# Tying the second layer's weight decoding to places in the product stream, and a reordered, two-queue ending, in a scan plus two-layer MLP kernel

## Chip, cores and metric

One core of one Trainium2 chip runs the whole program in one launch. The metric is the device time of one execution in microseconds (us); for the kernel before it is 641.49 us, the median of 3 runs (641.38 to 641.57).

## The reference

A decayed linear-attention scan over 4 sequences of 768 steps (8 heads of 32) gives 3072 tokens of 256 numbers. Two MLP layers follow:

```python
x = attn_out.transpose(0, 2, 1, 3).reshape(3072, 256)
xn = x / sqrt(mean(x * x, -1) + 1e-6) * rms_g          # layer 1, d_ff 1536
x = (silu(xn @ w_gate) * (xn @ w_val)) @ w_out
r = maximum(x @ w_in, 0.0)                              # layer 2, d_ff 2048
out = (s * (r * r) + b) @ w_out2
```

The weights arrive as 64-bit floats and are turned into fp32 on the chip ("decoding"). To keep fp32 accuracy on fast passes, both factors of a product are split into a high and a low part (`hi`, `lo`), and three products are summed.

## The kernel before, in words

The program is not issued as it is written. A recording class, `Plan`, collects every engine call with its predecessors; `issue` (L322) then sorts them by list scheduling with the planner's own prices and hands each engine its instructions in that order. So all work shows as line L356 in the profile, the warm-up products of TensorE as L352, and groups are told apart by tile names. Each engine then runs its list strictly in that order and waits by semaphores.

The stages: the scan runs in pairs of chunks (tiles `ab`, `a_sb`, `m`, `y`, `xn`, `ss`, `rs`, `xth`, `xtl`). Layer 1 works on 7 blocks of tokens (4, 4, 4, 5, 5, 5, 5 chunks of 96); for each block, 12 tiles `m` of the hidden width are made by `hidden1` (tiles `h`, `s`, `hi`, `lo`) and multiplied into the accumulators `o`. Block 0 uses plain fp32 products (`hidden1_plain`, weights `w1f`) while the weights of layer 1 are decoded by `decode1`. The 16 tiles of layer 2's weights are decoded by `decode2` (L715), called once for every third `m` of blocks 2 to 5 (L1039). One decoding of a layer-2 tile is five VectorE operations of 512 columns (`e<-raw`, `raw<-raw`, `w2f<-raw`, `e<-e,sg`, `w2f<-w2f,e`), two ScalarE operations (`e`, `sg`) and one GpSimd sum (`w_sum`). Nothing but data and buffers says when they run; the planner may put them before the place in the program text where they are called.

Layer 2 works on 6 groups of 512 tokens with seven products in place of eight (`seven`, `seven_out`, L923), which collect in seven accumulators of 256 columns in four PSUM banks (`soon`, `late`; tiles `acc` and `o`). At a group's end `seven_out` puts the seven together on VectorE into `res`, and `store` (L822) applies `s * ... + bias` to 512 columns on ScalarE into `ob` and sends the pieces to `out_t`, all on SyncE's queue (SP). The last group has six such stores.

TensorE's idle stretches at the start are filled by `issue` with products of constants (L352), so many as the planner's clock finds room for.

Of the kernel before, what the change touches and what calls it, by code (L numbers as in the profile page):

```python
# [8 lines left out]
F32 = mybir.dt.float32  # L9
# [7 lines left out]
AF = mybir.ActivationFunctionType  # L17
ALU = mybir.AluOpType

P = 128  # L20
# [5 lines left out]
SEQ = 768  # L26
CPB = SEQ // CH
UT = 2 * CH
NPAIR = 2
# [13 lines left out]
N2 = 512  # L43
# [14 lines left out]
class Plan:  # L58
# [23 lines left out]
    def __init__(self, nc):  # L82
        self.nc, self.ops, self.clock, self.pace = nc, [], 0.0, False
        self.seen, self.rings, self.masks, self.before, self.heads = {}, {}, {}, {}, {}
        self.closed, self.sent, self.turns, self.bundle = set(), None, False, None
        self.now_free = True
        self.fresh, self.after, self.held, self.squares = False, None, None, None
        for e in ("tensor", "vector", "scalar", "gpsimd", "sync"):
            setattr(self, e, Engine(self, e))

    def add(self, eng, fn, args, kw):
        op = dict(eng=eng, fn=fn, args=args, kw=kw, preds={}, paced=self.pace, i=len(self.ops))
        op["dur"] = self.price(eng, fn, args, kw)
        if fn == "dma_start":
            op["eng"] = self.DMA[eng]
        reads = [a for k, a in kw.items() if k not in self.WRITES] + list(args)
        writes = [a for k, a in kw.items() if k in self.WRITES]
        if args and fn in self.FIRST_OUT:
            writes.append(reads.pop(len(kw) - len(writes)))
        for a in reads:  # L100
            self.touch(op, a, False)
        for a in writes:
            self.touch(op, a, True)
        if self.turns:

            if self.sent is not None:
                op["preds"].setdefault(self.sent["i"], -self.DMA_LEAD - self.sent["dur"])
            self.sent = op
        if self.after is not None:
            op["preds"].setdefault(self.after, 0.0)  # L110
        op["clock"] = self.clock
        op["group"] = kw["out"].name if fn == "matmul" and not self.pace else None
        if self.fresh and op["eng"] == "tensor":
            op["dur"] += self.SWITCH[fn]
            self.fresh = False
        if self.bundle is not None and op["eng"] == "tensor":
            op["group"] = self.bundle
            self.join(op)
        if self.pace:
            self.clock += op["dur"]  # L120
        self.ops.append(op)


# [247 lines left out]
def scan_glu_relu2(ctx: ExitStack, tc: tile.TileContext, bc, xr, aa, cst, w1, w2, gn, sv, bv, out):  # L371
    nc = Plan(tc.nc)
    PS = bass.MemoryType.PSUM

    const = ctx.enter_context(tc.tile_pool(name="const", bufs=1))
# [9 lines left out]
    xt_p = ctx.enter_context(tc.tile_pool(name="xt", bufs=2))  # L385
    x1_p = ctx.enter_context(tc.tile_pool(name="x1", bufs=3))
    s_p = ctx.enter_context(tc.tile_pool(name="s", bufs=3))
    hl_p = ctx.enter_context(tc.tile_pool(name="hl", bufs=LAG + 1))
    ps_h = ctx.enter_context(tc.tile_pool(name="ps_h", bufs=2, space=PS))
    ps_o = ctx.enter_context(tc.tile_pool(name="ps_o", bufs=1, space=PS))  # L390
    ps_y = ctx.enter_context(tc.tile_pool(name="ps_y", bufs=2, space=PS))
# [1 line left out]
    cst_sb = const.tile([P, 4], F32, name="cst_sb")  # L393
    raw_bc = const.tile([P, 2, 3, 2 * R + NST], F32, name="raw_bc")
    a_sb = const.tile([P, SLOTS, NH, AW], F32, name="a_sb")
    sb = const.tile([P, 6], F32, name="sb")
    s_sb, b_sb, bias_sb, g_sb = sb[:, 0:1], sb[:, 1:2], sb[:, 2:4], sb[:, 4:6]
    delta = const.tile([P, NH, AW], F32, name="delta")
    ident = const.tile([P, P], F32, name="ident")
# [289 lines left out]
    def flat(t):  # L689
        return t.rearrange("p a b -> p (a b)")  # L690
# [24 lines left out]
    def decode2(m):  # L715
        raw = w2_p.tile([P, 4 * P], I64, tag="w2", name="raw2")
        words(raw, w2[m])
        w2f[m] = w2f_p.tile([P, 4, P], F32, tag="w2f", name="w2f")
        decode(raw, flat(w2f[m]), 4 * P)
        if m:  # L720
            last = w2f[0][:, 2:4] if m == 1 else w2_sum
            nc.gpsimd.tensor_tensor(out=w2_sum, in0=last, in1=w2f[m][:, 2:4], op=ALU.add)
# [96 lines left out]
                        if lo < hi:  # L819
                            yield lo - a, to + lo - at, hi - lo  # L820

    def store(g, t, o):  # L822
        res = s_p.tile([P, N2], F32, tag="s", name="ob")
        nc.scalar.activation(
            out=res, in_=o, func=AF.Identity, scale=s_sb, bias=bias_sb[:, t:t + 1]
        )
        todo = sorted(runs(g * N2, (g + 1) * N2))
        while todo:
            at, to, n = todo.pop(0)
            same = [r for r in todo if r[2] == n]  # L830
            more = []
            if same:
                step, jump = same[0][0] - at, same[0][1] - to
                while (at + (len(more) + 1) * step, to + (len(more) + 1) * jump, n) in todo:
                    more.append((at + (len(more) + 1) * step, to + (len(more) + 1) * jump, n))
                    todo.remove(more[-1])
            k = len(more) + 1
            src = res[:, at:at + n]
            dst = out[t * P:(t + 1) * P, to:to + n]
            if more:  # L840
                src = bass.AP(src.tensor, src.offset, [list(src.ap[0]), [step, k], [1, n]])
                dst = bass.AP(dst.tensor, dst.offset, [list(dst.ap[0]), [jump, k], [1, n]])
            nc.sync.dma_start(out=dst, in_=src)

    combined = {}

# [25 lines left out]
    def bias_products():  # L872
        ps = ps_y.tile([P, 2, 512], F32, tag="y", name="bias")
        ones = nc.nc.const_aps.tensor(1.0, (P, 2), F32)
        for t in range(2):
            nc.tensor.matmul(out=ps[:, t, 0:2], lhsT=w2_sum[:, t], rhs=ones, start=True, stop=True)
        for t in range(2):
            nc.vector.tensor_scalar_mul(bias_sb[:, t:t + 1], ps[:, t, 0:1], b_sb)

# [43 lines left out]
    def seven_out(j, q, parts):  # L923
        n = HALF
        if q == 0:
            o_t[j, 2] = new_sums(j)
        sums, soon, late = o_t[j, 2]
        last = q == F2 // 2 - 1
        for k, ((wh, wl), (hi, lo)) in enumerate(zip(combined[q], parts)):
            three(sums[k], wh, wl, hi, lo, q == 0 and k in (0, 2, 3, 5), last and k in (1, 2, 4, 6))  # L930
        if not last:
            return
        res = xt_p.tile([P, 4, n], F32, tag="xth", name="res")
        side = xt_p.tile([P, 2, n], F32, tag="xtl", name="side")
        two = slice(0, 4, 3)
        first, second, third = (
            t[:, 0:2 * n].rearrange("p (s n) -> p s n", s=2) for t in (soon[0], late[0], late[1])
        )
        one = soon[1][:, None, 0:n].to_broadcast([P, 2, n])
        nc.scalar.copy(out=side, in_=first)  # L940
        nc.vector.tensor_tensor(out=res[:, two], in0=one, in1=side, op=ALU.subtract)
        nc.vector.tensor_tensor(out=res[:, two], in0=second, in1=res[:, two], op=ALU.add)
        nc.vector.tensor_tensor(out=res[:, 0], in0=res[:, 0], in1=third[:, 0], op=ALU.subtract)
        nc.vector.tensor_tensor(out=res[:, 1], in0=third[:, 1], in1=side[:, 0], op=ALU.add)
        store(j, 0, res[:, 0:2].rearrange("p s n -> p (s n)"))
        nc.vector.tensor_tensor(out=res[:, 3], in0=third[:, 1], in1=res[:, 3], op=ALU.add)
        nc.vector.tensor_tensor(out=res[:, 2], in0=side[:, 1], in1=third[:, 0], op=ALU.subtract)
        store(j, 1, res[:, 2:4].rearrange("p s n -> p (s n)"))

    def drain(n):  # L950
        while len(pending) > n:
# [4 lines left out]
                      in_=aa.rearrange("c (u f) -> (c u) f", u=2))  # L956
# [7 lines left out]
        out=ident, in_=ident, compare_op=ALU.not_equal, fill=1.0, base=0,  # L964
# [70 lines left out]
    for i, (layer, j, m) in enumerate(plan):  # L1035
        if (layer, j) == (1, 1):
            split1(m)
        if layer == 1 and 2 <= j < NBLK - 1 and m % 3 == 0:
            decode2((j - 2) * 4 + m // 3)  # L1039
        late = m if layer == 1 and j == NBLK - 1 else F1 + m // 2 if (layer, j) == (2, 0) and m % 2 == 0 else None  # L1040
        if late == 0:
            split_rows(0)
            bias_products()
        for q in range(F2 // 2):
            if late == (max(2 * q, 1) if q < 7 else F1 + 2):
                combine(q)
        if layer == 2:
            if m == 0 and (g := j + 1) * N2 < 2 * NPAIR * SEQ:
                split_rows(g)
            if m % 2 == 0:  # L1050
                seven(j, m // 2)
                drain(LAG)
            continue
        hidden1(j, m)
        drain(LAG)
        for (i0, n0), (i1, n1) in zip(marks, marks[1:]):
            if i0 <= i < i1:
                tokens_to(n0 + -(-(n1 - n0) * (i + 1 - i0) // (i1 - i0)))
# [74 lines left out]
```

## Time and profile before

| | |
|---|---|
| median of 3 runs | 641.49 us |
| the profiled execution | 641.33 us |
| its span, first to last instruction | 639.2 us |
| TensorE matmul busy | 623.8 us (98%) |
| TensorE weight load busy | 555.5 us (87%) |
| VectorE (DVE) busy | 482.3 us (75%) |
| ScalarE (ACT) busy | 437.3 us (68%) |
| GpSimd (POOL) busy | 60.5 us (9%) |

The span is from the first to the last instruction; 2.1 us of the execution lie outside it. Matmuls are pipelined, so "busy" of TensorE (PE) counts stretches in which at least one is in flight; a lost moment shows as an idle time before a group or as a larger step from one start to the next. PEclk is the granted clock of TensorE as a share of full speed.

### The profile page before, as it was taken

The page shows a single profiled execution, that of the slowest core. Times are in us where ns is not written, and L with a number is a line of the kernel's source. Part 1 is how long each engine was busy: PE and PEld are TensorE (multiplying, and loading weights), DVE is VectorE, ACT ScalarE, POOL GpSimd, SP SyncE. Part 2 cuts the span into 40 slices and gives each one's busy share as a digit, 9 for nine tenths or more (in the row PEclk, how much of TensorE's full clock was granted, in tenths as well). Part 3 has the DMA queues.
Part 4 walks back from the last instruction along what each step waited for, and adds up shares of the span by engine and source line. Part 5 has one row for each costly group of instructions (what it writes and reads, how often), then busy time and mean ns, then how long its engine had stood idle before and what let it go on. Part 6 is the DMA issues. An engine that isn't in the chain of part 4 may idle for free.

```text
span 639.2 us, 12930 instructions
## 1 busy us (share of the span) xinstructions
PE 623.8 (98%) x4959; PEld 555.5 (87%) x4959; DVE 482.3 (75%) x979; ACT 437.3 (68%) x928; POOL 60.5 (9%) x88
## 2 busy tenths in 40 slices
PE   8899999999999999999999999999999999999995
PEld 7799999889988888888888888999999999999995
DVE  7999999999754635544554559787888888888794
ACT  4697566676644534553554569888889888888884
POOL 3000022235210000000001220000000000000000
PEclk9899999999999999999999999999999999999999
DMA  7868235553202203210100000001010010000101
GB/s 226 241 200 252 56 100 158 139 132 89 56 1 49 61 5 62 65 36 4 41 1 2 0 1 1 2 4 31 2 33 2 1 34 1 26 8 2 34 1 33
DMA packets 33694, 35.00 MB, mean 55 GB/s; under 512 B 14048, under 2 KB 30048, under 8 KB 33632
## 3 DMA queue, kind: packets, MB, share of 16 engines
q1 hardware_dynamic: 33376, 33.98, 20.2%
q8 instruction: 39, 0.64, 0.4%
q10 hardware_dynamic: 256, 0.20, 0.1%
q14 instruction: 23, 0.19, 0.1%
HBM read 30.90 MB, written 3.25 MB: 53 GB/s over the span
## 4 chain that ended last, share of the span: by engine, by line
PE 82%; DVE 11%; ACT 3%; issue 2%; DMA 0%; DVEq 0%; SPq 0%; ACTq 0%
PE h L356 46%; PE o L356 19%; PE acc L356 12%; PE y L356 4%; DVE w2f L356 2%; DVE e L356 2%; DVE s L356 1%; DVE lo L356 1%; DVE a_sb L356 1%; DVE raw L356 1%; DVE m L356 1%; DVE w1l L356 1%; PE o L352 1%; DVE xtl L356 1%; DVE w1f L356 1%
## 5 line engine op out<-in xcount | busy, mean ns | idle before, releaser
L356 ACT ACTIVATE s<-h 128x512 f32<-128x512 f32 (+2 forms) x168 | 96.2, 573 | 55.5 <-PE h L356 53.3
L356 ACT CAST hi<-s 128x256 fp32r<-128x256 f32 (+2 forms) x168 | 78.2, 473 | 69.2 <-DVE s L356 67.6
L356 PE MATMUL h<-x1h,w2h 128*128 128x512 f32 x384 | 119.5, 392 | 0.0
L356 DVE TENSOR_TENSOR lo<-s,hi 128x256 fp32r<-128x256 f32 (+2 forms) x168 | 87.9, 524 | 27.8 <-ACT hi L356 27.2
L356 PE MATMUL h<-xth,w1h 128*128 128x480 f32 (+1 forms) x288 | 107.2, 373 | 1.2 <-DVE s L356 0.8
L356 PE MATMUL h<-xtl,w1h 128*128 128x480 f32 (+1 forms) x288 | 106.6, 370 | 0.0
L356 PE MATMUL h<-xth,w1l 128*128 128x480 f32 (+1 forms) x288 | 106.4, 369 | 0.0
L356 PE MATMUL acc<-hi,w2c 128*128 128x256 f32 x448 | 82.4, 281 | 0.0
L356 DVE TENSOR_TENSOR s<-h,s 128x480 f32<-128x480 f32 (+1 forms) x72 | 44.5, 618 | 49.6 <-PE h L356 45.6
L356 PEld LDWEIGHTS h<-x1h,w2h 128*128 128x128 f32 x384 | 69.0, 188 | 11.8
L356 PE MATMUL h<-x1l,w2h 128*128 128x512 f32 x192 | 75.1, 391 | 0.0
L356 PEld LDWEIGHTS acc<-hi,w2c 128*128 128x128 f32 x448 | 71.6, 190 | 2.7
L356 DVE TENSOR_TENSOR added<-s 128x256 f32<-128x256 f32 x144 | 57.1, 421 | 10.0 <-ACT s L356 9.2
L356 PE MATMUL acc<-lo,w2c 128*128 128x256 f32 x224 | 63.2, 282 | 0.0
L356 PEld LDWEIGHTS h<-xth,w1h 128*128 128x128 f32 x288 | 54.1, 188 | 9.6 <-DVE s L356 2.6
L356 ACT ACTIVATE s<-s 128x512 f32<-128x512 f32 x96 | 59.6, 632 | 1.1
L356 PEld LDWEIGHTS h<-xtl,w1h 128*128 128x128 f32 x288 | 54.1, 188 | 6.3 <-issue 1.0
L356 PEld LDWEIGHTS h<-xth,w1l 128*128 128x128 f32 x288 | 54.1, 188 | 6.0 <-issue 0.3
L356 DVE TENSOR_TENSOR lo<-added,hi 128x768 fp32r<-128x768 f32 x48 | 46.0, 958 | 14.5 <-ACT hi L356 14.4
L356 PE MATMUL o<-hi,w1h 128*128 128x480 f32 (+1 forms) x144 | 53.2, 369 | 0.5 <-ACT hi L356 0.5
L356 PE MATMUL o<-lo,w1h 128*128 128x480 f32 (+1 forms) x144 | 52.7, 366 | 0.8 <-DVE lo L356 0.8
L356 PE MATMUL o<-hi,w1l 128*128 128x480 f32 (+1 forms) x144 | 53.2, 369 | 0.0
(98 smaller groups left out, 1099.6 us busy)
## 6 DMA issues: line engine op xcount, KB each, us to landing
raw<-in_w SPq DMA_DIRECT2D x12, 768.0 KB, 5.1
raw<-in_w SPq DMA_DIRECT2D x16, 512.0 KB, 4.3
a_sb<-a_scr SPq DMA_DIRECT2D x28, 196.0 KB, 4.2
xh<-in_xr SPq DMA_DIRECT2D x60, 48.0 KB, 1.9
raw_bc<-in_bc SPq DMA_DIRECT2D x56, 32.0 KB, 2.2
raw_bc<-in_bc SPq DMA_DIRECT2D x112, 16.0 KB, 2.6
out_t<-ob SPq DMA_DIRECT2D x14, 96.0 KB, 1.8
out_t<-ob SPq DMA_DIRECT2D x6, 144.0 KB, 1.9
```

What stands on the lines that cost most here:

```text
L352: self.nc.tensor.matmul(out=idle, lhsT=ones, rhs=ones, start=True, stop=True)
L356: getattr(engine, op["fn"])(*op["args"], **op["kw"])
```

## The change

1. A call of `decode2` sets `nc.floor` to the last product recorded before it (`nc.latest`, set only for the layers' products). While it is set, every VectorE and ScalarE operation gets that product as a predecessor, so no part of a decoding on these two engines can be planned before its place among layer 1's products. Loads and GpSimd sums are not tied.
2. At a group's end ScalarE scales first and VectorE adds last: four ScalarE operations of 256 columns write `s * part + bias` into `res`, and four `scalar_tensor_tensor` operations add `+s` or `-s` (the new column `minus_s`) times the last two accumulators. `ob` and its two ScalarE operations of 512 columns are gone; stores read `res`, which gets a pool of its own.
3. The last group's second half is stored from ScalarE's queue in place of SyncE's.

```diff
+        self.now_free, self.floor, self.latest = True, None, None
...
-        if self.after is not None:
-            op["preds"].setdefault(self.after, 0.0)
+        for i in (self.after, self.floor if eng in ("vector", "scalar") else None):
+            if i is not None:
+                op["preds"].setdefault(i, 0.0)
...
         if self.pace:
             self.clock += op["dur"]
+            self.latest = op["i"]
...
+    res_p = ctx.enter_context(tc.tile_pool(name="res", bufs=1))
...
-    sb = const.tile([P, 6], F32, name="sb")
+    sb = const.tile([P, 7], F32, name="sb")
+    minus_s = sb[:, 6:7]
...
-    def store(g, t, o):
-        res = s_p.tile([P, N2], F32, tag="s", name="ob")
-        nc.scalar.activation(
-            out=res, in_=o, func=AF.Identity, scale=s_sb, bias=bias_sb[:, t:t + 1]
-        )
+    def store(g, t, res):
+        queue = nc.scalar if t and (g + 1) * N2 == 2 * NPAIR * SEQ else nc.sync
...
-            nc.sync.dma_start(out=dst, in_=src)
+            queue.dma_start(out=dst, in_=src)
...
+        nc.vector.tensor_scalar(out=minus_s, in0=s_sb, scalar1=-1.0, scalar2=None, op0=ALU.mult)
...
-        res = xt_p.tile([P, 4, n], F32, tag="xth", name="res")
+        res = res_p.tile([P, 4, n], F32, tag="res", name="res")
...
-        nc.vector.tensor_tensor(out=res[:, 0], in0=res[:, 0], in1=third[:, 0], op=ALU.subtract)
-        nc.vector.tensor_tensor(out=res[:, 1], in0=third[:, 1], in1=side[:, 0], op=ALU.add)
-        store(j, 0, res[:, 0:2].rearrange("p s n -> p (s n)"))
-        nc.vector.tensor_tensor(out=res[:, 3], in0=third[:, 1], in1=res[:, 3], op=ALU.add)
-        nc.vector.tensor_tensor(out=res[:, 2], in0=side[:, 1], in1=third[:, 0], op=ALU.subtract)
-        store(j, 1, res[:, 2:4].rearrange("p s n -> p (s n)"))
+        parts = [(side[:, 0], 1, s_sb), (res[:, 0], 0, minus_s), (side[:, 1], 0, minus_s), (res[:, 3], 1, s_sb)]
+        for k in (2, 1, 0, 3):
+            t = 0 if k < 2 else 1
+            nc.scalar.activation(
+                out=res[:, (1, 0, 2, 3)[k]], in_=parts[k][0], func=AF.Identity, scale=s_sb, bias=bias_sb[:, t:t + 1]
+            )
+        for t in range(2):
+            for k in (2 * t, 2 * t + 1):
+                to = res[:, (1, 0, 2, 3)[k]]
+                nc.vector.scalar_tensor_tensor(
+                    out=to, in0=third[:, parts[k][1]], scalar=parts[k][2], in1=to, op0=ALU.mult, op1=ALU.add
+                )
+            store(j, t, res[:, 2 * t:2 * t + 2].rearrange("p s n -> p (s n)"))
...
         if layer == 1 and 2 <= j < NBLK - 1 and m % 3 == 0:
+            nc.floor = nc.latest
             decode2((j - 2) * 4 + m // 3)
+            nc.floor = None
```

The planner sorts everything anew with these predecessors, so the order changes in places that the diff does not touch. Three places follow.

First, VectorE at the start of the program, from the first `w1f` weights to the second (`raw_135` of before is `raw_138` of the change, the second tile; `a_sb<-ab` is the scan of a chunk, `m<-y` a scan product, `h` the hidden tile of block 0). Before:

```order
L356 TENSOR_TENSOR w1f<-w1f,e 128x768
L356 SCALAR_TENSOR_TENSOR a_sb<-ab,delta 128x392
L356 TENSOR_SCALAR raw_135<-raw_135 128x768
L356 TENSOR_SCALAR e<-raw_136 128x768
L356 TENSOR_TENSOR e<-e,sg 128x768
L356 TENSOR_TENSOR h_154<-h,h_154 128x192
L356 SCALAR_TENSOR_TENSOR w1f<-raw_135 128x768
L356 TENSOR_TENSOR m<-y,a_sb 128x8x48
L356 TENSOR_SCALAR raw_136<-raw_136 128x768
L356 TENSOR_TENSOR w1f<-w1f,e 128x768
```

And now:

```order
L358 SCALAR_TENSOR_TENSOR a_sb<-ab,delta 128x392
L358 TENSOR_TENSOR e<-e,sg 128x768
L358 COPY held<-rs 128x2
L358 SCALAR_TENSOR_TENSOR w1f<-raw_137 128x768
L358 TENSOR_SCALAR e<-raw_138 128x768
L358 TENSOR_TENSOR w1f<-w1f,e 128x768
L358 TENSOR_SCALAR raw_138<-raw_138 128x768
L358 TENSOR_SCALAR e<-raw_139 128x768
L358 TENSOR_TENSOR e<-e,sg 128x768
L358 SCALAR_TENSOR_TENSOR w1f<-raw_138 128x768
L358 TENSOR_TENSOR w1f<-w1f,e 128x768
L358 TENSOR_TENSOR h_157<-h,h_157 128x192
```

The scan now stands ahead of the first weights, and `h`, `m` and a mask of the third tile stand behind the second. On TensorE the constant products ahead of the first transposes (`y<-ident,xn`) grow from 23 to 31, and 12 new ones stand between the first tile's products and the second's; from the products `y<-xh,m` of the next pair on, TensorE's list is for a while the old one.

Second, VectorE among layer 1's products (`s`, `lo` are the pair that `hidden1` needs of it for each tile, `xtl` a scan result, `w2h` a split of a decoded tile). Before, at the last tiles of block 1:

```order
L356 TENSOR_TENSOR w2h<-w2f,w2h 128x256
L356 TENSOR_TENSOR s<-h,s 128x384
L356 TENSOR_TENSOR e<-e,sg 128x512
L356 TENSOR_SCALAR raw_585<-raw_585 128x512
L356 SCALAR_TENSOR_TENSOR xtl<-y,sb,xth 128x2x48 x2
L356 TENSOR_TENSOR w2h<-w2f,w2h 128x256
L356 TENSOR_TENSOR lo<-s,hi 128x384
L356 SCALAR_TENSOR_TENSOR xtl<-y,sb,xth 128x2x48 x2
L356 SCALAR_TENSOR_TENSOR w2f<-raw_585 128x512
L356 TENSOR_SCALAR raw_616<-raw_616 128x512
```

And now, at the end of block 2 (its last `s`, `lo` of 384 columns):

```order
L358 TENSOR_TENSOR s<-h,s 128x384
L358 TENSOR_SCALAR e<-raw_487 128x512
L358 TENSOR_TENSOR lo<-s,hi 128x384
L358 TENSOR_SCALAR raw_487<-raw_487 128x512
L358 SCALAR_TENSOR_TENSOR w2f<-raw_487 128x512
L358 TENSOR_TENSOR e<-e,sg 128x512
L358 TENSOR_TENSOR w2f<-w2f,e 128x512
L358 TENSOR_TENSOR s<-h,s 128x480
L358 TENSOR_TENSOR lo<-s,hi 128x480
L358 TENSOR_TENSOR s<-h,s 128x480
L358 TENSOR_TENSOR lo<-s,hi 128x480
L358 TENSOR_TENSOR s<-h,s 128x480
```

Of the 16 decodings none stands before block 2 now: there is one for every third `hi`/`lo` pair, from the 12th pair to the 57th, where before all 16 stood between the 2nd pair and the 21st.

Third, ScalarE's last rows, before:

```order
L356 COPY side<-acc 128x512
L356 ACTIVATE ob<-res,sb 128x512 x2
```

And now:

```order
L358 COPY side<-acc 128x512
L358 ACTIVATE res<-side,sb 128x256 x2
L358 ACTIVATE res<-res,sb 128x256 x2
L358 DMA out_t<-res 128x32
L358 DMA out_t<-res 128x2x96
L358 DMA out_t<-res 128x2x144
```

Two of the four scalings need only `side`; the other two need the sum of VectorE's second addition. ScalarE issues its three stores behind its last scaling. VectorE's last four rows, `res<-o_1467,sb,res 128x256`, work on the third, first, second and fourth quarter of `res` in this order; SyncE keeps three stores.

## Rows read from the trace of the kernel before

**Rows 1.** Busy time by stretch: us, then busy us (count) by engine, PEclk, DMA share, GB/s.

```profile
100.00:180.00 80.00, 77.43 (x758) 70.37 (x758) 74.65 (x158) 54.91 (x140) 30.68 (x28) 1.00 0.44 110
180.00:320.00 140.00, 140.00 (x1247) 117.41 (x1247) 68.86 (x137) 63.34 (x157) 5.03 (x8) 1.00 0.17 37
420.00:632.00 212.00, 212.00 (x1351) 192.52 (x1350) 177.73 (x356) 182.16 (x339) 0.00 (x0) 1.00 0.05 13
```

**Rows 2.** Waits of PE from 100 to 180 us: total, times, longest.

```profile
PE h L356 <- DVE s L356: 0.8, 2, 0.4
PE o L356 <- DVE lo L356: 0.8, 1, 0.8
PE o L356 <- ACT hi L356: 0.5, 1, 0.5
```

**Rows 3.** Timeline of PE around one such wait: start, duration, operation, idle before.

```profile
122.02 0.34 PE L356 MATMUL o<-hi,w1l 128*128 128x384 f32 x1
122.20 0.33 PE L356 MATMUL o<-lo,w1h 128*128 128x384 f32 x1
123.04 0.44 PE L356 MATMUL o<-hi,w1h 128*128 128x384 f32 x1 [0.50 <-ACT hi L356]
```

**Rows 4.** Groups of DVE from 80 to 165 us, the decodings: busy, mean ns, idle before.

```profile
L356 DVE SCALAR_TENSOR_TENSOR w2f<-raw 128x512 f32<-128x512 uint32 x16 | 11.2, 698 | 0.0
L356 DVE TENSOR_TENSOR w2f<-w2f,e 128x512 f32<-128x512 f32 x16 | 11.0, 690 | 0.0
...
L356 DVE TENSOR_SCALAR raw<-raw 128x512 int32<-128x512 int32 x15 | 7.2, 477 | 0.0
...
L356 DVE TENSOR_TENSOR e<-e,sg 128x512 bf16<-128x512 bf16 x16 | 6.6, 413 | 0.0
L356 DVE TENSOR_SCALAR e<-raw 128x512 uint16<-128x512 uint16 x15 | 6.3, 417 | 0.0
```

**Rows 5.** Timeline of DVE at the start: three operations between first and second weights.

```profile
15.46 0.97 DVE L356 TENSOR_TENSOR_SCAN a_sb<-ab,delta 128x392 f32<-128x392 f32 x1
...
17.73 0.35 DVE L356 TENSOR_TENSOR h<-h,h 128x192 f32<-128x192 f32 x1
...
18.86 0.55 DVE L356 TENSOR_TENSOR m<-y,a_sb 128x384 f32<-128x384 f32 x1
```

**Rows 6.** Timeline of PE at the start: the groups that waited.

```profile
20.89 1.54 PE L356 MATMUL h<-xth,w1f 128*128 128x192 f32 x8 [1.01 <-DVE w1f L356]
24.14 1.12 PE L356 MATMUL y<-xh,m 64*64 64x32 f32 x32 [1.71 <-DVE m L356]
...
33.20 2.87 PE L356 MATMUL h<-xth,w1f 128*128 128x192 f32 x16 [0.54 <-ACT xth L356]
```

**Rows 7.** Busy time by stretch at the start, columns as in rows 1.

```profile
12.00:16.00 4.00, 3.25 (x43) 2.76 (x41) 3.97 (x8) 3.83 (x9) 0.27 (x1) 1.00 0.83 187
20.00:24.00 4.00, 1.54 (x8) 1.27 (x8) 4.00 (x7) 2.53 (x4) 0.00 (x0) 1.00 0.74 226
26.00:30.00 4.00, 4.00 (x40) 3.94 (x37) 2.91 (x7) 2.18 (x7) 1.33 (x1) 0.57 1.01 232
```

**Rows 8.** Timeline of the end, all engines, after the last but one addition.

```profile
631.43 0.69 DVE L356 TENSOR_TENSOR res<-o,res 128x512 f32<-128x512 f32 x1
...
632.92 1.53 ACT L356 ACTIVATE ob<-res,sb 128x512 f32<-128x512 f32 x2 [2.34 <-DVE res L356]
633.13 0.41 DVE L356 TENSOR_TENSOR res<-side,o 128x256 f32<-128x256 f32 x1
633.76 3.00 SPq L356 DMA_DIRECT2D out_t<-ob  x6
```

**Rows 9.** A group of DVE with a pointer scalar, by form (mean ns after the comma).

```profile
L356 DVE SCALAR_TENSOR_TENSOR xtl<-y,sb,xth 128x96 fp32r<-128x96 f32 x56 | 14.4, 310 | 6.6 <-ACT xth L356 6.2
```

**Rows 10.** DMA issues: count, KB each, median us from issue to landing.

```profile
out_t<-ob SPq DMA_DIRECT2D x14, 96.0 KB, 1.8
...
xh<-in_xr ACTq DMA_DIRECT2D x4, 48.0 KB, 3.1
```

More of the change, by code (lines that the diff above doesn't have):

```diff
@@ L85, in __init__ @@
         self.closed, self.sent, self.turns, self.bundle = set(), None, False, None
-        self.now_free = True
+        self.now_free, self.floor, self.latest = True, None, None
         self.fresh, self.after, self.held, self.squares = False, None, None, None
```

## Prediction

> **What bounds the kernel now.** I read the page first: TensorE (PE) matmuls cover 98% of the span, so only what PE waits for, and what stands before its first and behind its last product, can move the time. Then busy time by stretch [rows 1]. From 180 to 320 us and from 420 to 632 us PE is busy all the time, with VectorE (DVE) at 49% (68.86 of 140) in the one and 84% (177.73 of 212) in the other. From 100 to 180 us it loses 2.57 us, and there DVE is full (74.65 of 80). Then PE's list of waits for that stretch [rows 2]: it waits for `s` and `lo` of DVE and `hi` of ScalarE (ACT), the three steps by which `hidden1` hands a tile on. Last the start [rows 5 to 7] and the end [rows 8].
>
> **Middle: the decodings move.** What fills DVE in that stretch is the decoding of layer 2's weights: five operations a tile, 0.698 + 0.690 + 0.477 + 0.413 + 0.417 = 2.70 us, 16 tiles, about 43 us from 80 to 165 us [rows 4]. `hidden1`'s own steps queue among them, as the order before shows. With the floor these 43 us leave the stretch up to block 2 and come back as one tile at every third `hi`/`lo` pair, up to the end of block 5.
>
> What it gives: the waits of rows 2 sum to 0.8 + 0.8 + 0.5 = 2.1 us in four waits. Idle time understates a wait, because matmuls overlap: the step from 122.20 to 123.04 is 0.84 us, while 0.50 is listed as idle and the regular step there is 0.18 (122.02 to 122.20), so 0.84 − 0.50 − 0.18 = 0.16 comes on top [rows 3]. So 2.1 + 4 × 0.16 = 2.7 us. Of the 0.47 us idle that these four do not hold (2.57 − 2.1) I count 0.4 as curable: 3.1 us at most. All of it goes if DVE is no longer full.
>
> What it costs: where the decodings go, DVE had 49%. About 12 tiles fall between 180 and 320 us: 12 × 2.70 = 32 us, which makes (68.86 + 32) / 140 = 72%. In layer 2 DVE runs at 84% and ACT at 86% and PE loses nothing [rows 1]; that is the cover. If it fails, one decoding can cost what one wait for `s` costs, 0.4 + 0.16 = 0.56 us [rows 2, 3]. I put two such brushes in, 0.3 us after what slack hides. Middle: **−2.8 us**, between −3.1 and −1.0.
>
> GpSimd's sums (`w_sum`) move with the decodings; it has 31 us of work in 80 [rows 1], and the chain that ends in it is wanted only when layer 2 starts. The 16 loads of raw tiles on SyncE's queue (SP) move too, behind the same buffers; SP waits there, and nothing but loads stands behind them. `minus_s` is one column. All three at nothing.
>
> **Start: a by-product.** The planner's new order puts the scan of 0.97 us ahead of the first weights [rows 5], so the first products come up to 0.97 us later; constant products fill the gap. Between the first and the second weights the scan, `h` (0.35) and `m` (0.55) are gone [rows 5]: 1.87 us less, so the second weights come at least 1.87 − 0.97 = 0.9 us sooner, and the wait of 1.01 us for them at 20.89 us [rows 6] nearly closes. But PE's next group, at 24.14 us, waits 1.71 us for `m` of DVE [rows 6], and up to there DVE has the same work in both orders and no idle time (4.00 of 4 busy from 20 to 24) [rows 7]. So PE is no earlier there: 0, with +0.7 and −0.2 as bounds.
>
> What can change is the clock. From 26 to 30 us it stands at a mean of 0.57 of full, after PE had been busy for 1.54 us of the 4 from 20 to 24 [rows 7]; that is (1 − 0.57) / 0.5 × 4 = 3.4 us at half speed, 1.2 GHz in place of 2.4. It costs at most 1.7 us of products. After 3.25 of 4 (81%, constant products included, 12 to 16 us) it had stayed up [rows 7]. In the new order PE's second group comes some 1.3 us sooner, 12 constant products run before it, and the spread `ab` and the first `o` products follow it: I count some 2.8 us busy of the 4 from 20 to 24, 70%, nearer to the 81% than to the 39%. I take it that the clock stays up. The half-speed products lie on the chain to the wait at 33.20 us (`h`, the ACT steps behind it, the transposes, `xth`) [rows 6]; from there DVE is nearly full again and gives part back. Of 0 to −1.7 I take the middle: **−0.8 us**.
>
> **End.** Before [rows 8]: the second addition ends at 631.43 + 0.69 = 632.12 us; four additions follow on DVE, up to 633.13 + 0.41 = 633.54; two scalings of 512 columns on ACT, 1.53 us from 632.92 on; then six stores on SP from 633.76 to 636.76, 0.50 each, and 2.47 us later the span ends. Now:
>
> - ACT scales the first two quarters while DVE adds; these are hidden. The scaling of `res` (first and fourth quarter) starts at 632.12. A scaling of 256 columns was not seen; it lies between 0.38 (half of 1.53 / 2) and 0.77 us. It has half the columns but the same start-up; I take 0.55. They end at 632.7 and 633.2.
> - DVE's four `scalar_tensor_tensor` of 256 columns: like the addition, 0.41 [rows 8], plus something for the pointer. The nearest row with one takes 0.310 us for 96 columns [rows 9], so 160 columns more, at 0.41 / 256 us each at most, give 0.57 as the upper end. I take 0.45, 0.40 from start to start. The first quarter waits for ACT (632.7), so the four end at 632.6, 633.15, 633.55 and 633.95.
> - SP stores from 633.2: third issue at 634.2, done 634.7. ACT's queue starts behind its last scaling, 633.25; its third store waits for 633.95 and is done at 634.75. Both are done some 2.0 us before 636.76.
>
> If a store on ACT's queue lands as on SP's (1.8 us [rows 10]), the span ends 2.0 us sooner. The only row for ACT's queue has 3.1 us [rows 10], at the start, with the DMA engines busy; that would take 1.3 back. I take the row for the same stores, and 0.1 for issuing from two engines: **−1.9 us**, between −0.6 and −2.2.
> The Trainium skill (DMA: Bandwidth & Descriptors, "Issuing engines are not separate DMA queues") says that DMAs from all engines run on the same 16 DMA engines, and that several issuing engines only save the time of issuing, "usually small relative to the DMA itself". By its first half ACT's stores land like SP's, and the sum keeps −1.9; by ACT's own row it would be −0.6. Its second half does not fit here: six issues in a row took 3.00 us, against 1.8 for a landing [rows 8, 10].
>
> At the other five group ends the same operations run beside PE, which loses nothing there; ACT has some 4 × 0.55 in place of 1.53 us each time, 0.7 us more a group: nothing. Cover: the 14% that ACT is idle; without it, 5 × 0.7 = 3.5 us.
>
> **Sum** on the profiled execution (641.33 us, span 639.2): −2.8 − 0.8 − 1.9 = −5.5, so 635.8 us. The median of the runs is 0.16 us above that execution; I leave it out.
>
> **Rivals.**
>
> 1. *The clock falls as before.* For it: PE still waits for `m` shortly before 24.14 us. Then the start gives 0: 636.6 us.
> The Trainium skill (TensorE: Matmul & The Clock Gate, Part 1) has the throttled state as the default, which activity lifts, and says that the moment of change varies from run to run. By that rule the fall may stay in some runs and not in others; the granted clock here shows one fall after a thin stretch.
> 2. *The middle was not the decodings'.* `s`, `hi` and `lo` also queue behind scans, `xtl` and splits, which stay. If two thirds of the waits remain, the middle gives 1.0: 637.6 us.
> 3. *A new wait at every decoding (slower).* The five operations now stand beside blocks 2 to 5 at 16 fixed places, ahead of `s` or `lo` in DVE's list; the order shows one `e<-raw` between `s` and `lo`. If each place costs PE one wait of 0.56 us, that is 9.0 us against 3.1 + 0.8 + 1.9 = 5.8 of gains: 644.5 us. It decides from 5.8 / 16 = 0.36 us a place on. Against it: 84% of DVE without a wait in layer 2.
> 4. *The end does less than it says.* ACT's queue is slow to land, or the last scaling holds ACT's stores back: −0.6 there, 637.1 us.
>
> **How the numbers follow.** Forecast 0.45; rival 1 0.25; rival 2 0.12; rival 4 0.11; rival 3 0.07. The range: below, the forecast with every term near its good end (3.1 + 1.7 + 2.2 = 7.0, so 634.3); above, rivals 1 and 2 together, 638.4. That leaves out rival 3 and the worst sums. A measurement of this kernel can tell about 0.2% (1.3 us) from no change. All cases but rival 3 are faster by more; of rival 3's 0.07 some 0.02 end within the 1.3 us, and sums of two rivals add 0.03 there: faster 0.90, same 0.05, slower 0.05.
>
> **What would show it.** Middle: PE busy all of 100 to 180 us, no wait for `s`, `hi`, `lo`, DVE under 85% there and above 65% from 180 to 320; rival 3 shows as waits for `s` or `lo` beside `w2f` rows from 160 to 310. Start: granted clock 1.00 from 26 to 30; the group that waited at 33.20 some 0.8 us sooner. End: from the second addition's end to the span's end 5.2 us in place of 7.1, with stores on two queues. I would be wrong if PE's waits in the middle stay with DVE no longer full, or if the second addition is no longer what the end hangs on.

## The result, and the profile after

The changed kernel takes 633.81 us (median of 4 runs, 633.74 to 633.88) against 641.47 us (641.38 to 641.57): ratio 0.9883, 95% interval 0.9867 to 0.9898. The forecast was 635.8 us, with 634.3 as the lower end. So it was right that it is faster, but the gain is 7.7 us in place of 5.7, half a microsecond below the range.

I cut both traces at three products of TensorE (PE): the first with `w1h` (layer 1's high part), the first with `w2h` (layer 2) and the last one. Timeline of PE, before:

```profile
77.77 0.47 PE L356 MATMUL h<-xth,w1h 128*128 128x384 f32 x1
...
377.30 0.40 PE L356 MATMUL h<-x1h,w2h 128*128 128x512 f32 x1
```

and after:

```profile
78.04 0.47 PE L358 MATMUL h<-xth,w1h 128*128 128x384 f32 x1
...
371.64 0.40 PE L358 MATMUL h<-x1h,w2h 128*128 128x512 f32 x1
```

| stretch (us) | before | after | difference | forecast |
|---|---|---|---|---|
| start, to the first `w1h` product | 77.77 | 78.04 | +0.27 | −0.8 |
| middle, `w1h` to `w2h` | 299.53 | 293.60 | −5.93 | −2.8 |
| layer 2, to the last product | 254.51 | 254.32 | −0.19 | 0 |
| end, from the last product on | 7.42 | 5.86 | −1.56 | −1.9 |
| span | 639.23 | 631.82 | −7.41 | −5.5 |

The middle gained twice what was forecast; the start gained nothing. Before, four products of block 0 (`o<-h,w1f`) come behind the first cut that now come ahead of it; cut at block 0's last product, with the same work on both sides, the two differences are +0.19 and −5.85. The middle in busy time by stretch, columns as in [rows 1]:

```profile
100.00:180.00 80.00, 80.00 (x785) 75.18 (x784) 56.96 (x124) 49.51 (x128) 6.27 (x9) 1.00 0.35 83
180.00:320.00 140.00, 140.00 (x1262) 117.42 (x1261) 95.42 (x194) 78.71 (x190) 19.34 (x23) 1.00 0.26 63
```

PE has no idle time left from 100 to 180 us (2.57 before), and the list of PE's waits for that stretch, [rows 2] before, is empty. VectorE (DVE) falls from 74.65 to 56.96 of 80 us and rises from 68.86 to 95.42 of 140 (68%; 72% was forecast). GpSimd (POOL) falls with it, from 30.68 to 6.27 us. Groups of DVE and POOL by form, 80 to 165 us; first before:

```profile
L356 DVE TENSOR_TENSOR lo<-s,hi 128x384 fp32r<-128x384 f32 x22 | 15.1, 685 | 0.0
...
L356 POOL TENSOR_TENSOR w_sum<-w_sum,w2f 128x256 f32<-128x256 f32 x13 | 17.8, 1372 | 38.9 <-DVE w2f L356 38.8
```

then after (`w_sum` there from 80 to 330 us):

```profile
L358 DVE TENSOR_TENSOR lo<-s,hi 128x384 fp32r<-128x384 f32 x23 | 12.7, 552 | 6.3 <-ACT hi L358 6.3
...
L358 POOL TENSOR_TENSOR w_sum<-w_sum,w2f 128x256 f32<-128x256 f32 x14 | 12.9, 924 | 118.6 <-DVE w2f L358 118.6
```

The same `lo` took 685 ns on the mean before and 552 after. I had not looked at this before the result. In the trace of before, 16 of the 22 took 541 to 556 ns and six took 996 to 1092. In each of those six a `w_sum` of GpSimd was already under way when `lo` began; `lo` ended some 0.42 us after that sum. One of them, in the timelines of DVE, POOL and PE before:

```profile
118.86 0.96 DVE L356 TENSOR_TENSOR_SCAN a_sb<-a_sb,delta 128x392 f32<-128x392 f32 x1
119.74 1.03 DVE L356 TENSOR_TENSOR lo<-s,hi 128x384 fp32r<-128x384 f32 x1
120.69 0.96 DVE L356 TENSOR_TENSOR_SCAN a_sb<-a_sb,delta 128x392 f32<-128x392 f32 x1
121.58 0.39 DVE L356 TENSOR_TENSOR w2h<-w2f,w2h 128x256 fp32r<-128x256 f32 x1
121.89 0.55 DVE L356 TENSOR_TENSOR s<-h,s 128x384 f32<-128x384 f32 x1
...
118.67 1.69 POOL L356 TENSOR_TENSOR w_sum<-w_sum,w2f 128x256 f32<-128x256 f32 x1
```

`w_sum` runs from 118.67 to 120.36; `lo` starts at 119.74 and takes 1.03 us in place of 0.55. The scan, the split (`w2h`) and the next `s` stand behind it in VectorE's list, and the `hi` made from that `s` is what PE waits for at 123.04 [rows 3]. The Trainium skill (SBUF — State Buffer, "Who interferes with whom") has a rule for such a wait: VectorE and GpSimd share a pair of ports as an exclusive lock, an operation with both inputs in SBUF takes part in it, and the one that comes second waits until the first is done. The trace agrees (0.62 us from the start of `lo` to the end of the sum, and 0.41 from there to its own end, in the rows above). But a sum's recorded start does not tell who came first: in three of the 16 others (90.85, 135.31 and 151.39 us) a sum's row also began 0.11 to 0.17 us ahead of `lo`, and there the sum took 2.6 to 3.1 us and `lo` its 0.55:

```profile
135.20 3.14 POOL L356 TENSOR_TENSOR w_sum<-w_sum,w2f 128x256 f32<-128x256 f32 x1 [5.50 <-DVE w2f L356]
135.31 0.55 DVE L356 TENSOR_TENSOR lo<-s,hi 128x384 fp32r<-128x384 f32 x1
```

The start, by stretch as in [rows 7]:

```profile
20.00:24.00 4.00, 3.34 (x25) 2.48 (x22) 4.00 (x9) 2.12 (x4) 0.00 (x0) 1.00 0.80 235
26.00:30.00 4.00, 4.00 (x42) 3.71 (x41) 3.23 (x7) 2.28 (x8) 1.33 (x1) 0.61 0.77 181
```

and the groups of PE that answer to [rows 6]:

```profile
24.65 1.12 PE L358 MATMUL y<-xh,m 64*64 64x32 f32 x32 [1.30 <-DVE m L358]
...
33.62 0.59 PE L358 MATMUL h<-xth,w1f 128*128 128x192 f32 x2 [0.45 <-ACT xth L358]
```

PE was busy for 3.34 us of the 4 from 20 to 24, more than the 2.8 I counted, and the clock fell all the same (0.61 in place of 0.57). The group that was to come 0.8 us sooner than 33.20 came at 33.62.

The end, all engines, as [rows 8]:

```profile
624.99 0.69 DVE L358 TENSOR_TENSOR res<-o,res 128x512 f32<-128x512 f32 x1 [0.60 <-PE o L358]
...
625.71 1.09 ACT L358 ACTIVATE res<-res,sb 128x256 f32<-128x256 f32 x2 [0.93 <-DVE res L358]
...
625.96 0.28 PE L358 MATMUL o<-lo,w2c 128*128 128x256 f32 x1
626.70 1.66 DVE L358 SCALAR_TENSOR_TENSOR res<-o,sb,res 128x256 f32<-128x256 f32 x4 [1.02 <-ACT res L358]
627.22 1.61 ACTq L358 DMA_DIRECT2D out_t<-res  x3
627.60 1.35 SPq L358 DMA_DIRECT2D out_t<-res  x3
```

The second addition now ends at 625.68, before PE's last product has started. DVE's first of four starts 0.46 us behind that product's end (625.96 + 0.28). Its row names ACT, whose event came last; but this first operation works on the third quarter, which ACT scaled first of all, from `side` alone, so of the two the product is what it still lacked. So the end hangs on that product.

### The profile page after: what moved, and what is told of

It reads as the page before. It is cut to its first block, busy times and chain, and to the rows that moved or that the text cites. A ratio compares the mean times of both kernels' runs of the same rounds, so it can differ in the third digit from the quotient of the medians.

```text
span 631.8 us, 12985 instructions
## 1 busy us (share of the span) xinstructions
PE 621.4 (98%) x4979; PEld 556.4 (88%) x4979; DVE 484.2 (77%) x980; ACT 446.2 (71%) x940; POOL 50.6 (8%) x88
## 4 chain that ended last, share of the span: by engine, by line
PE 95%; DVE 2%; ACT 1%; issue 0%; DVEq 0%
PE h L358 54%; PE o L358 22%; PE acc L358 13%; PE y L358 5%; PE o L354 1%; DVE w1f L358 1%; DVE e L358 0%; ACT xn L358 0%; PE ab L358 0%; DVE res L358 0%; DVE a_sb L358 0%; DVE xh L358 0%; ACT e L358 0%; ACT xth L358 0%; ACT xh L358 0%
## 5 line engine op out<-in xcount | busy, mean ns | idle before, releaser
L358 DVE TENSOR_TENSOR lo<-s,hi 128x256 fp32r<-128x256 f32 (+2 forms) x168 | 85.7, 511 | 30.0 <-ACT hi L358 27.2
L358 DVE TENSOR_TENSOR added<-s 128x256 f32<-128x256 f32 x144 | 56.4, 419 | 13.5 <-ACT s L358 12.5
```

What stands on the lines that cost most here:

```text
L358: getattr(engine, op["fn"])(*op["args"], **op["kw"])
```

## The experiments

On the chips of the experiments the kernel before itself ran between 639.0 and 643.7 us, with mean granted clocks from 0.999 to 0.991. So I judge the middle by its stretch in the trace, not by the whole time. That stretch repeats well: 299.53 and 299.54 in two traces of the old order; 293.2, 293.2, 293.4, 293.4, 293.6 and 294.2 in six of the new one.

### Which part of the change: floor and end apart

e1 is the kernel before with the floor alone; e2 the changed kernel without this line:

```diff
-            nc.floor = nc.latest
```

> The kernel before with the floor alone; end, store queues and the res buffer stay as before. The open question is the stretch from the first w1h product to the first w2h product, which got 5.9 us shorter (299.5 to 293.6) where 2.8 was forecast. If the floor alone does it, this stretch is 293.6 +-0.5 and the whole 636.0 (641.5 - 5.9 + 0.4 or less at the start). If the other parts of the change (the res buffer off the xth ring, ob off the s ring) give half of it, the stretch is some 296.5 and the whole 638.5.

> The changed kernel without the floor: new end, two store queues, res buffer, but the decodings free to run early. If the floor alone shortened the middle: stretch 299.5 +-0.7, last product to the end 5.9 us, whole 639.9 (641.5 - 1.6). If the other parts share in the middle: stretch 296.5, whole 637.

e1: middle 294.03, end 7.27; 635.96 us, ratio 0.9906 (0.9881 to 0.9930). e2: middle 298.63, end 5.51; 636.86 us, 0.9929 (0.9903 to 0.9954). So the floor makes the middle (−5.5 of −5.9) and the new end makes the end. The whole of e2 was 3 us under its expectation. Middle and end account for 1.3 us of that (298.63 for 299.5, 5.51 for 5.9). The rest goes with the start's clock, below: three of its six runs had mean clocks of 0.998 or more (635.6 to 636.0 us), and the other three, at 0.994 to 0.996, took 637.7 to 639.0.

### What fills VectorE: GpSimd's sums, or too much work

e3 keeps the order of before on every engine and thins the sums, so that the bias sum is left out but for one column in each half:

```diff
+            cut = P if m == 1 else 1
+            nc.gpsimd.tensor_tensor(out=w2_sum[:, :, 0:cut], in0=last[:, :, 0:cut], in1=w2f[m][:, 2:4, 0:cut], op=ALU.add)
```

> The kernel before with its order of instructions on every engine unchanged, but GpSimd's w_sum additions cover 1 of 128 columns per half from the second on (the bias sum is left out but for one column). Theory A, VectorE is full because all decodings stand in one stretch: VectorE stays over 90% busy from 80 to 165 us, at most 1.5 us are gained (640.0 to 641.5). Theory B, GpSimd's sums running beside VectorE lengthen its operations (lo from 549 to up to 1092 ns) and that makes PE wait: lo's mean falls to 550 ns and 3 to 5 us of the middle's 5.9 go (636.5 to 638.5).

e5 keeps it too, leaves the sums whole, and thins one of DVE's five operations when it is issued; 504 of its 512 columns are left out, so most of the decoded weights lack that step:

```diff
+            if op["eng"] == "vector" and op["fn"] == "tensor_tensor" and kw["out"].dtype == BF16 and kw["out"].free_size() == 512:
+                op["kw"] = dict(kw, out=kw["out"][:, 0:8], in0=kw["in0"][:, 0:8], in1=kw["in1"][:, 0:8])
```

> The kernel before with its order unchanged; of each layer-2 decoding VectorE's e<-e,sg covers 8 of 512 columns (so the decoded weights are wrong but for those), which takes some 16 x 0.35 = 5.6 us off VectorE between 80 and 165 us. GpSimd's sums stay whole. Theory A, what counts is that VectorE has no moment free: it gains like the thin sums did, the stretch from the first w1h to the first w2h product is 294.5 to 295.5. Theory B, what counts is that GpSimd's sums stretch single lo steps to twice their time: lo's mean stays near 680 ns and half or more of the waits stay, the stretch is 297 to 299.5.

`lo` from 80 to 165 us, of e3 and of e5:

```profile
L356 DVE TENSOR_TENSOR lo<-s,hi 128x384 fp32r<-128x384 f32 x23 | 12.5, 545 | 0.5 <-ACT hi L356 0.5
```

```profile
L359 DVE TENSOR_TENSOR lo<-s,hi 128x384 fp32r<-128x384 f32 x22 | 15.1, 686 | 0.0
L359 DVE TENSOR_TENSOR e<-e,sg 128x8 bf16<-128x8 bf16 x16 | 3.0, 185 | 0.0
```

e3: middle 294.85, so 4.7 of the 5.9 us come back with no decoding moved (637.01 us, 0.9931, 0.9907 to 0.9955). `lo` is shorter by 22 × 0.14 = 3.1 us there, `ss` by 4 × (0.571 − 0.166) = 1.6 and `raw` by 15 × (0.477 − 0.418) = 0.9: 4.7 for 5.6 us, 0.84 us per us. e5: 297.10; 16 × (0.413 − 0.185) = 3.6 us less work on DVE give 2.4, with `lo` at 686 as before (638.91 us, 0.9965, 0.9949 to 0.9980); which other operations are held up shifts (`e<-raw` takes 1.6 us more, `ss` and `raw` 1.7 less), with little in sum. Theory B's numbers hold in both. But B alone is too narrow: plain work taken off gives some 0.67 us per us. DVE had no free moment (84.73 of 85 us busy before; 81.36 in e3). So I read it that whatever lengthened its queue, a held-up `lo` or a decoding, reached PE.

### A held-up `lo` where VectorE has room

In the changed kernel, 20 extra GpSimd additions start with `lo` (e7, reading `hi`) or ahead of it (e13, 384 columns, reading `s`):

```diff
+                    self.nc.gpsimd.tensor_tensor(out=extra, in0=extra, in1=op["kw"]["out"][:, 0:384], op=ALU.add)
```

> The changed kernel with its order unchanged on the other engines and 20 extra GpSimd additions of 128x256 fp32, each starting when ScalarE's hi of the 2nd to 21st pair is written, that is together with lo on VectorE. lo's mean rises from 552 ns to between 700 and 1100, GpSimd's additions from 735 to about 1350. Theory A, a stretched lo costs only where VectorE has no free time: the stretch from the first w1h to the first w2h product stays at 293.6 to 294.3. Theory B, a stretched lo makes PE wait by itself: over 295.

> The changed kernel with its order unchanged on the other engines and 20 extra GpSimd additions of 128x384 fp32, each starting when VectorE's s of the 2nd to 21st pair is written, so that it is under way when lo comes to its turn. At least 10 of the 23 lo between 80 and 165 us take 0.7 to 1.1 us in place of 0.55. If a held-up lo costs only where VectorE's queue has no free time, the stretch from the first w1h to the first w2h product stays at 293.2 to 294.2. If it costs by itself, each of the ten or more takes 0.3 us or more: over 296.

`lo` and the additions, 80 to 165 us, of e7 and of e13:

```profile
L358 DVE TENSOR_TENSOR lo<-s,hi 128x384 fp32r<-128x384 f32 x23 | 13.7, 597 | 6.2 <-ACT hi L358 6.2
...
L363 POOL TENSOR_TENSOR extra<-extra,hi 128x256 f32<-128x256 f32 x20 | 20.4, 1019 | 53.3 <-ACT hi L358 51.8 <-ACT xh L358 1.4
```

```profile
L358 DVE TENSOR_TENSOR lo<-s,hi 128x384 fp32r<-128x384 f32 x22 | 18.2, 828 | 6.1 <-ACT hi L358 6.0
```

Timelines of e13 around PE's largest wait in the middle:

```profile
153.24 1.33 POOL L363 TENSOR_TENSOR extra<-extra,s 128x384 f32<-128x384 f32 x1 [3.52 <-DVE s L358]
153.60 1.25 DVE L358 TENSOR_TENSOR e<-e,sg 128x512 bf16<-128x512 bf16 x1
...
155.24 0.98 DVE L358 SCALAR_TENSOR_TENSOR xtl<-y,sb,xth 128x96 fp32r<-128x96 f32 x4
...
155.87 0.53 PE L358 MATMUL y<-raw_bc 32*64 32x128 f32 x4 [0.69 <-issue]
```

e7 did not decide: where `lo` begins first, it keeps its 0.55 us and the addition waits (1.03 to 1.12 us in place of the 0.73 that `w_sum` takes undisturbed); only two `lo` were held up, middle 293.98. That trace is of the fastest of its four runs (634.86 us, 632.48 to 637.87; 0.9901, 0.9864 to 0.9938); all four had mean clocks of 0.998 or more, and what the others lost is not shown. In e13 13 of 22 were held up (0.93 to 1.30 us), some 6 us in all, and two `e<-e,sg` by another 1.65. The middle is 295.44: 1.2 to 2.3 us more than the six traces above, between the two expectations. That largest wait, the last row above, has no releaser in the profile, but it ends 0.10 us after one of the four `xtl`, which read `y`, and these stand behind an `e` of 1.25 us in place of 0.42. So in this trace a microsecond of hold-up costs 0.15 to 0.3 us, against 0.84 before. By whole times, taken with the same hold-up, it is 0.2 to 0.6: e13 (635.02 us, 0.9897, 0.9876 to 0.9918) took 633.69 to 636.03 us in its three runs at clocks of 0.998 or more, e15 beside it 631.25 to 632.21. That a hold-up costs less where DVE has room fits both, but rests on one trace and few runs.

### Where the cover ends

Extra DVE operations of 512 fp32 columns on a scratch tile, 40 in number, from the 2nd to the 21st `s`/`lo` pair: one behind `s` and one behind `lo` (e4), or both behind `lo` (e6). In e12 each of the decodings' 80 operations has one extra of about its own length behind it.

```diff
+                    for n in ((512,), (512,))[name == "lo"]:
+                        self.nc.vector.tensor_tensor(out=extra[:, 0:n], in0=extra[:, 0:n], in1=extra[:, 0:n], op=ALU.max)
```

> The changed kernel with its order unchanged, and 40 extra VectorE operations of 512 fp32 columns on a scratch tile from the 2nd to the 21st s/lo pair of layer 1 (one behind each s, one behind each lo), some 25 us in the stretch from 80 to 165 us; nothing extra on GpSimd. It fills VectorE again (58 + 25 = 83 of 85 us). Theory A: PE waits for s, lo and hi come back there, 3 to 6 us are lost: 637 to 640. Theory B: VectorE's queue alone costs little: under 1 us, 633.8 to 634.8.

> The same 40 extra VectorE operations as in e4 (512 fp32 columns, 28 us), but both behind lo and none between s and lo. Theory A, the total load of VectorE in the stretch decides: it loses as e4 did, the stretch from the first w1h to the first w2h product is 299 to 301. Theory C, the delay of the single step decides (an operation between s and lo stands in the hand-on of a tile, one behind lo doesn't): it is 294 to 296.5.

> The changed kernel with its order unchanged, and each of the 80 VectorE operations of the 16 decodings followed by one more of about the same length on a scratch tile: 5.4 us a place in place of 2.7, VectorE at some 92 to 95% from 180 to 320 us. It asks where the cover ends. If VectorE's free time is all that matters, the loss is under 1.5 us: 293.6 to 295 from the first w1h to the first w2h product. If a place costs PE one wait as soon as a run of VectorE's work stands ahead of s, as rival 3 priced it (0.56 us a place), it is 16 x 0.56 = 9 us: 300 to 305.

Waits of PE (60 to 330 us) in e6, then in e12, with e12's busy time by stretch:

```profile
PE h L358 <- DVE s L358: 3.3, 4, 1.3
...
PE y L358 <- issue: 3.3, 3, 1.4
...
PE h L358 <- ACT s L358: 1.2, 1, 1.2
...
PE y L358 <- DVE m L358: 1.0, 2, 0.8
```

```profile
180.00:320.00 140.00, 137.03 (x1152) 114.00 (x1151) 110.76 (x226) 74.78 (x177) 20.13 (x20) 1.00 0.26 63
...
PE h L358 <- DVE s L358: 3.6, 6, 1.1
PE y L358 <- DVE m L358: 1.6, 5, 0.5
```

e4: middle 300.00 (639.70 us, 0.9969, 0.9952 to 0.9986). e6: 306.14 (646.75 us, 1.0082, 1.0059 to 1.0104). e12: 306.13 (644.91 us, 1.0042, 1.0024 to 1.0060). In none of them is DVE full: 75.14 and 70.80 of 85 us in e4 and e6, 110.76 of 140 (79%, not the 92 to 95 expected) in e12. My theory A (busy share) falls with e6, and so does C: two operations behind `lo` cost 12.5 us, twice what one behind `s` and one behind `lo` do (6.4). Some half of the loss are waits for `s` (or ScalarE's step ahead of it) to free the bank of `h`, of which there are two. The other half are waits of the scan's products: for `m`, or with no releaser, ending 0.10 us after an `xtl` that reads `y`. PE's steps over 0.45 us from start to start sum to 7.2 us at `h` and 6.0 at `y` in e6, 6.8 and 6.4 in e12, 2.1 and 3.5 in e4; in each, one step of 0.5 at `h` stands in the changed kernel too. So I read it that the run of work ahead of the next step that PE waits for decides, be it `s`, `m` or `xtl`. One decoding at every third pair is absorbed in the pairs after it; two are not (12.5 us over 16 places, 0.78 us each, more than either expectation).

### The start's clock

e8 and e14 are the changed kernel, e9 the kernel before, with constant products in the gap ahead of the scan products that wait for `m` (20 of them; 28 in e9):

```diff
+                    for _ in range(20):
+                        self.nc.tensor.matmul(out=idle, lhsT=zeros, rhs=ones, start=False, stop=False)
```

> The changed kernel with 20 more constant products on PE (of zeros, some 1.1 us) in the idle time of 1.30 us ahead of the scan products that wait for m at 24.65 us. If the thin stretch from 22 to 26 us is why the granted clock falls to half at 26 us, the clock stays at 1.00 from 26 to 34 us and the first w1h product comes 1 to 3 us sooner (76 to 77 in place of 78.0 to 79.5). If the clock falls for another reason, the clock falls at 26 to 27 us as before and nothing is gained, or up to 0.2 us is lost.

> The kernel before with 28 more constant products on PE (of zeros, some 1.5 us) in its idle time of 1.71 us ahead of the scan products that wait for m at 24.14 us; nothing else. If the clock falls because of that thin stretch, in this order too, the granted clock is 1.00 from 24 to 36 us and the whole is 638.5 to 639.8 (641.4 less 1.7 to 2.9). If the changed kernel needs its own order of the start for that (its second weights come sooner), the clock falls as before and the whole stays at 641.4 +-0.5.

> The kernel of e8 (the changed one with 20 products of zeros ahead of the scan products at 24.65 us) once more, beside the changed kernel on one chip. If the fill keeps the clock up, all its runs have a mean granted clock of 0.998 or more and the whole is 631.5 to 632.5. If the chip did it, its runs spread like those of the changed kernel.

> The changed kernel, beside e14 on one chip. If the fill is what keeps the clock up: mean granted clocks of 0.992 to 0.997 and 633.5 to 634.5. If the chip does it: as e14.

> The changed kernel unchanged, on the chip of the experiments, so that the others can be set beside it. The first w1h product at 78 to 79.5 us by how long the clock stays down, the middle 293.6, the end 5.5 to 5.9; whole 633.8 to 635.5.

By stretch, as in [rows 7]: e14, then e15 beside it on the same chip.

```profile
22.00:24.00 2.00, 2.00 (x26) 1.89 (x25) 2.00 (x5) 1.09 (x3) 0.00 (x0) 1.00 0.48 161
...
28.00:30.00 2.00, 2.00 (x13) 1.83 (x13) 1.97 (x5) 1.94 (x6) 1.11 (x1) 1.00 1.13 135
```

```profile
22.00:24.00 2.00, 0.69 (x6) 0.40 (x4) 2.00 (x5) 1.09 (x3) 0.00 (x0) 1.00 0.28 84
...
28.00:30.00 2.00, 2.00 (x8) 2.00 (x7) 1.50 (x3) 1.06 (x3) 1.34 (x1) 0.50 1.10 175
```

| kernel | us | ratio (95%) | mean clock of its runs | first `w1h` product (us) |
|---|---|---|---|---|
| e9, before + fill | 639.96 | 0.9974 (0.9965 to 0.9983) | 0.996 to 0.998 (10 runs) | 76.39 |
| e8, after + fill | 631.92 | 0.9855 (0.9831 to 0.9878) | 0.998 to 0.999 (4) | 76.34 |
| e14, the same | 632.29 | 0.9859 (0.9844 to 0.9874) | 0.998 to 0.999 (4) | 76.35 |
| e10, after | 634.08 | 0.9886 (0.9872 to 0.9899) | 0.992 to 0.997 (4) | 78.44 |
| e15, after | 631.94 | 0.9861 (0.9840 to 0.9881) | 0.993, 0.998, 0.999, 1.000 | 78.55 |

With the fill no run's mean clock fell below 0.996, in either order (e9 ends 0.2 us above its expectation). The mean also holds the fall behind the last products: e9's trace has 1.00 from 5.7 to 633.7 us and a mean of 0.997. Of the runs without a trace the time tells: all ten of e9 took 640.40 us or less, and 19 of the 20 runs of the kernel before beside them 641.04 or more. Without the fill the changed kernel sometimes keeps its clock (three of four runs in e15, 631.25 to 632.21 us, against 634.10 in the one at 0.993); e7 kept it without a fill too, with PE busy for 2.74 us of the 4 from 20 to 24, less than the 3.34 after which it fell in the trace above. So e15 missed its expectation, and e14 beside it does not tell the fill from the chip; e9, and e8 beside the kernel before (2 of its 13 runs at 0.998 or more), do. The fill does not beat a run that keeps the clock by itself: it makes that run the usual one. At a kept clock the first `w1h` product comes at 76.4 us in the old order and 76.3 in the new (block 0's last product at 82.0 and 81.8 to 82.2): the new order of the start is worth nothing by itself. Against the changed kernel the fill gains some 2 us only where the clock would fall (e10), and nothing in e15's median.

### The second queue

e11 stores all six pieces from SyncE's queue:

```diff
-        queue = nc.scalar if t and (g + 1) * N2 == 2 * NPAIR * SEQ else nc.sync
+        queue = nc.sync
```

> The changed kernel with all six last stores on SyncE's queue. If the second queue is worth what the sum gave it (three issues of 0.50 us taken off the row of six), the time from the last product to the end grows by 1.0 to 1.5 us to 6.9 to 7.3. If a store on ScalarE's queue is slow to land or ScalarE's last scaling holds it, the second queue was worth little: +0.3 or less.

End 6.58 us against 5.87 in e10 on the same chip: 0.7 us, between the two expectations (634.23 us, 0.9881, 0.9863 to 0.9898; in the whole time it drowns in the clock). On one queue the sixth issue is done 4.1 us after the last product's start, in place of 3.0 (628.95 − 625.96) on two. That is 1.1 us later, but the last landing, which ends the span, comes only 0.7 us later.

## Why the prediction was right and wrong, by its own steps

**What bounds the kernel: right.** In the middle PE waited only from 100 to 180 us, and these waits are gone.

**Middle, −2.8 forecast, −5.93 measured: the term was mis-sized, and its mechanism was incomplete.** What was incomplete is the step that put GpSimd's "31 us of work in 80" at nothing. The sums were more than half of the matter: e3 gets 4.7 us by thinning them alone. The spread of `lo`, 541 to 1092 ns for one shape, stood in the trace of before and I read no more than who waited for it. This alone would not have moved the sum, since decodings and sums leave the stretch together. The size was lost in the upper bound of 3.1 us. It took four waits and 0.16 us beside the idle time of each. The trace of before has eight in the middle; their steps from start to start sum to 5.30 us against 8 × 0.18 of regular steps, so 3.9 us, and the products after a restart have steps of 0.28 in place of 0.18 (some 1.0 in all such steps). The remaining 1 us lies in small differences of many steps and is not placed. With every wait counted in this way the bound would have been near 5 us.

**The cover: right in the result, wrong in the reason.** I argued that DVE at 84% in layer 2 costs nothing, so 72% here is safe. The places did hold, but e12 loses 12.5 us at 79%. Rival 3's price of 0.56 us a place was near (0.78 in e12, 12.5 / 20 = 0.63 in e6). I take it that the two pairs without a decoding behind each place kept it away; no run changed that spacing.

**Start, −0.8 forecast, +0.27 measured: the step "I take it that the clock stays up" failed.** Rival 1 came true, with its time too high by what the middle gave. Two stretches of one trace (39% busy ahead of a fall, 81% without one) were no ground: in the profiled run it fell after 84%, and in e7 it stayed up after 69%. The rule of the Trainium skill named with that rival (TensorE: Matmul & The Clock Gate, Part 1) is that the moment of change varies from run to run. The traces agree: in those of the changed kernel the fall begins at 26.9, 25.2 (e10) and 25.5 us (e15). The size was fair: a kept clock brings the first `w1h` product 1.4 us forward against a fall of 3.4 us (e9 against the kernel before) and 2.2 us against one of 6.8 (e14 against e15).

**End, −1.9 forecast, −1.56 measured.** From the second addition's end it is 6.14 us (631.82 − 625.68) against 5.2 forecast and 7.1 before. The step that failed is that DVE's four follow the second addition: that addition now ends 0.56 us before PE's last product does, and DVE's first starts 0.46 us behind the product. In e2, e4, e6, e12 and e13 the end is 5.50 to 5.55, with DVE's first 0.35 us sooner after the last product (e4); that is the forecast size, reached by another chain than the one forecast. Why it is late in the others stays open. The second queue gave 0.7 us (e11).

**Layer 2 at nothing: right** (−0.19 us); four scalings a group end in place of two cost nothing there.

## What to carry to other kernels

Where a planner or a floor moves work off one engine, look at who else moves with it: the longest and the median time of one operation in a group tell of a held-up engine, while the mean and the busy share hide it. A busy share does not tell whether a place has cover; what counts is the longest run of work ahead of the step that frees a buffer, and the pairs left to catch up. Price a wait by the step from start to start and the step after it, and count all of them, also those that list little idle time.

## What the runs showed of the hardware

`lo`, an operation of VectorE with both inputs in SBUF, took 0.93 to 1.30 us in place of 0.55 in 21 cases in which a GpSimd addition was under way at its start (six before, two in e7, 13 in e13). It kept its 0.55 in four others, three before and one in e7, in which the addition's row began 0.11 to 0.17 us ahead of it; the record does not tell why. It was not lengthened when it began first (0.56 us in e7); the GpSimd addition then took 1.03 to 1.12 us in place of 0.73. `s` of the same 384 columns, whose one input lies in PSUM, took 525 to 558 ns in every case before, beside sums or not. Even the `ss` of two columns took 0.70 to 0.72 us in place of 0.16 behind a sum.

The granted clock at the start fell in some runs and not in others of the same kernel on the same chip (e15, by the trace of one run and the mean clocks and times of the others). With 20 or 28 products of zeros in one gap (1.1 and 1.6 us from the first one's start to the last one's) it stayed up in all 18 runs, as three traces and the times of the other 15 show.
